# A fused causal attention and expert kernel: score arithmetic, transposes, PSUM banks and the order of the attention rounds changed

## The chip, the cores and the metric

The program runs on one core of a Trainium2 chip. The metric is the device time of one execution in microseconds, the median of three. A second number, the span, is the time from the first to the last instruction of one profiled execution; the rows below belong to that execution.

## The reference

```python
# q, k, v: (4, 12, 448, 64) fp32; w_in: (768, 2048), w_out: (2048, 768), a: (4,), b: (2,)
scores = 1/sqrt(64) * q @ k^T          # causal mask: -1e9 above the diagonal
attn   = exp(scores - max); attn /= sum(attn) + 1e-9
x      = (attn @ v), heads joined      # (1792, 768)
h      = x @ w_in                      # (1792, 2048)
P      = a0 + a1*h + a2*h^2 + a3*h^3
Q      = 1 + |b0|*|h| + |b1|*h^2
out    = (P / (Q + 1e-6)) @ w_out      # (1792, 768)
```

The expert weights arrive as 64-bit floats (the kernel reads them as pairs of 32-bit words) and are converted on the chip.

## The kernel before

**Attention.** Two heads form a pair `p`; there are 24 pairs (4 batches of 6). The work on a pair is cut into small tasks, and the table `ORDER` writes out one round of the attention: the name of a task, a part number, and `@lag`, the number of pairs by which it trails the round. `attend(p, plan)` runs the table once per round, from round -2 on. Each engine gets its instructions in the order in which the table issues them, so the table sets what each engine waits behind. The tasks are:

- `ld`, `lv`: loads of q, k and v through SP's queue. `q` and `k` transpose them on PE (L237, L254) into PSUM; `qh`, `kh` on ACT and `ql`, `kl` on DVE take them out as a high and a low fp32r part.
- `s.0` to `s.3` (`stage_b_pe`, L274): scores of four query blocks, each as three fp32r products (high by high, high by low, low by high). `s.0`, `s.1`, `s.2` make one product per head with 64 rows of the array (widths 128, 256, 384); `s.3` takes the last 64 queries of both heads together with all 128 rows (width 448).
- `m.i` on DVE (mask and row maximum), `e.i` on ACT (exponential with its row sum), `r` on DVE (reciprocal of the sums), `n.i` on POOL (normalisation of `E`, two sets of buffers).
- `c.0` to `c.3` (`c_pe`, L330): 16 transposes of normalised `E` tiles with all 128 rows; `a.n` (ACT) or `v.n` (DVE) copies each of the four results out, 512 columns at a time.
- `d.c` (`stage_d`, L353): fp32 products with v, 64 output columns of the array per head, 1024 columns a head in all; `dh`, `dl` write the high and low part of `x`.
- `cv` (`conv`): converting weights, two DVE and two POOL steps per item; 14 items (`NC`) are converted during the attention and the other 18 later, one per unit of the expert part.

**PSUM.** `ps_t` holds four banks in rotation for all transposes and for `d`; `ps_s` holds four in rotation for the scores.

**Expert part.** 64 units, each `p1` (18 products into `psH`), an elementwise chain on ACT and DVE, and `p2` (products into `psO` and `psM`). The list `TAIL` is the hand-written passage from the last rounds to the first units `p1.0` to `p2.0`; a loop over units follows.

Of the kernel before, what the change touches and what calls it, by code (L numbers as in the profile page):

```python
# [18 lines left out]
e.0 m.1 m.2 e.1 v.0@2 cv.3 k@-1 n.0@1 ld@-2 n.4@1 m.3 lv@1 e.2 n.3@1 n.6@1 s.3 cv.2@-1 qh@-1 a.3@2 kh@-1 s.2  # L19
n.2@1 n.1@1 d.0@2 e.3 m.6 m.4 d.3@2 n.5@1 e.6 m.5 e.4 ql@-1 d.1@2 d.2@2 cv.0@-2 dh@2 c.2@1 e.5 kl@-1 dl@2 c.1@1  # L20
cv.1@-2 s.0@-1 s.1@-1 a.2@1 c.0@1 m.0@-1 c.3@1 q@-2 r a.1@1
# [3 lines left out]
NHEAD = -2  # L25
# [12 lines left out]
def kernel(  # L38
# [27 lines left out]
    NC = 14  # L66
# [123 lines left out]
    def p1(t):  # L190
# [3 lines left out]
        for n, (w, x) in enumerate(((wih, xh), (wih, xl), (wil, xh))):  # L194
            for c in range(KD):
# [8 lines left out]
    raw, K, AT, pv, SUM, REC, psa, pss, psc, nmx, msk, xf = {}, {}, {}, {}, {}, {}, {}, {}, {}, {}, {}, {}  # L204

    def stage_load(p):
# [4 lines left out]
        t = raw[p]["q"] = ld.tile([P, 3, 2, D], F32, tag="q", name="qraw")  # L211
        for j in range(2):
            src = q[b, 2 * hp + j]
            nc.sync.dma_start(out=t[:, :, j], in_=src[:3 * P].rearrange("(c p) d -> p c d", p=P))
            nc.sync.dma_start(out=Q6[p % 2][half(j), j], in_=src[3 * P:])
        t = raw[p]["k"] = ld.tile([CP, NB, 2, D], F32, tag="k", name="kraw")
        for j in range(2):
            nc.sync.dma_start(
                out=t[:, :, j], in_=k[b, 2 * hp + j].rearrange("(c p) d -> p c d", p=CP)
            )  # L220

    def stage_load_v(p):
        b, hp = divmod(p, HP)
        t = V[p % 2]
        for j in range(2):
# [4 lines left out]
            out=t[:QB, :, 3], in_=v[b, 2 * hp:2 * hp + 2, 3 * P:].rearrange("j p d -> p j d")  # L230
# [55 lines left out]

    def stage_b_max(p, i):
# [5 lines left out]
        s = pss[p, i][:, :w]  # L293
# [21 lines left out]
    def stage_b_norm(p, i):  # L315
        e = E[p % 2][i][:, :b_w[i]]
# [396 lines left out]
```

## Time and profile before

| what | us |
|---|---|
| time, median of 3 (lowest, highest) | 667.59 (667.17, 668.99) |
| the profiled execution, its own time | 666.24 |
| its span | 664.5 |
| PE busy, share of the span | 644.9, 97% |
| DVE busy | 536.4, 81% |
| ACT busy | 431.9, 65% |
| POOL busy | 217.7, 33% |

Busy times are averages over stages with different limits; the rows further down take the attention, the passage and the expert part apart. PE is TensorE's matmul side, PEld its weight loads, DVE VectorE, ACT ScalarE, POOL GpSimd, SP the engine that issues the transfers.

### The profile page before, as it was taken

The page shows a single profiled execution, that of the slowest core. Times are in us where ns is not written, and L with a number is a line of the kernel's source. Part 1 is how long each engine was busy: PE and PEld are TensorE (multiplying, and loading weights), DVE is VectorE, ACT ScalarE, POOL GpSimd, SP SyncE. Part 2 cuts the span into 40 slices and gives each one's busy share as a digit, 9 for nine tenths or more (in the row PEclk, how much of TensorE's full clock was granted, in tenths as well). Part 3 has the DMA queues.
Part 4 walks back from the last instruction along what each step waited for, and adds up shares of the span by engine and source line. Part 5 has one row for each costly group of instructions (what it writes and reads, how often), then busy time and mean ns, then how long its engine had stood idle before and what let it go on. Part 6 is the DMA issues. An engine that isn't in the chain of part 4 may idle for free.

```text
span 664.5 us, 11697 instructions
## 1 busy us (share of the span) xinstructions
PE 644.9 (97%) x3960; PEld 541.6 (82%) x3960; DVE 536.4 (81%) x1060; ACT 431.9 (65%) x944; POOL 217.7 (33%) x271
## 2 busy tenths in 40 slices
PE   5999999999989999999999999999999999999997
PEld 3767767767658888788888888889999999999996
DVE  3899999999649999999999968767885666885654
ACT  4798999989766665555656657554564455665453
POOL 3677877785827552243554210000000000000000
PEclk9899999999999999999999999999999999999999
DMA  7679877898507989788696888754757775747753
GB/s 186 168 188 230 234 184 216 197 256 217 169 24 253 311 314 359 267 292 282 231 327 238 283 308 307 265 191 174 273 168 253 249 244 207 256 172 247 258 209 118
DMA packets 111675, 154.91 MB, mean 233 GB/s; under 512 B 71936, under 2 KB 84224, under 8 KB 111616
## 3 DMA queue, kind: packets, MB, share of 16 engines
q1 hardware_dynamic: 111616, 154.17, 71.0%
q8 instruction: 31, 0.51, 0.3%
q14 instruction: 28, 0.23, 0.1%
HBM read 117.18 MB, written 36.96 MB: 232 GB/s over the span
## 4 chain that ended last, share of the span: by engine, by line
PE 71%; DVE 19%; issue 5%; POOL 2%; ACT 2%; SPq 0%; DMA 0%; DVEq 0%; ACTq 0%; POOLq 0%
PE psH L196 23%; PE psO L511 16%; PE psM L512 8%; PE psS L282 8%; PE psD L359 6%; PE psC L340 5%; DVE u L138 3%; DVE p L471 3%; DVE p L465 3%; DVE whl L179 2%; DVE w L462 2%; DVE w L440 2%; POOL e L317 2%; DVE p L443 2%; PE psA L257 1%
## 5 line engine op out<-in xcount | busy, mean ns | idle before, releaser
L196 PE MATMUL psH<-xh,whl 128*128 128x512 f32 (+1 forms) x768 | 175.8, 364 | 0.0
L511 PE MATMUL psO<-whl,gh 128*128 128x512 f32 x448 | 160.4, 394 | 2.3 <-ACT gh L477 2.3
L196 PEld LDWEIGHTS psH<-xh,whl 128*128 128x128 f32 x768 | 136.0, 188 | 15.4 <-issue 0.3
L512 PE MATMUL psM<-whl,gh 128*128 128x256 f32 x448 | 126.2, 282 | 0.0
L317 POOL TENSOR_SCALAR e<-e,r 128x128 f32<-128x128 f32 (+3 forms) x168 | 95.9, 590 | 39.2 <-PE psC L340 20.8
L511 PEld LDWEIGHTS psO<-whl,gh 128*128 128x128 f32 x448 | 84.0, 188 | 22.8 <-ACT gh L477 5.8
L455 ACT ACTIVATE u<-w,lnb 128x512 f32<-128x512 f32 (+1 forms) x64 | 43.0, 672 | 90.6 <-DVE w L440 90.6
L302 ACT ACTIVATE e<-psS,nm 128x128 f32<-128x128 f32 (+3 forms) x168 | 83.2, 507 | 12.8 <-DVE sums L310 5.3
L196 PE MATMUL psH<-xl,whl 128*128 128x512 f32 (+1 forms) x384 | 87.5, 362 | 0.0
L512 PEld LDWEIGHTS psM<-whl,gh 128*128 128x128 f32 x448 | 84.6, 189 | 1.0
L295 DVE CUSTOM_DVE_ANT_0 psS<-psS,mask 128x128 f32<-128x128 f32 (+3 forms) x168 | 73.7, 467 | 11.5 <-PE psS L282 10.3
L511 PE MATMUL psO<-whl,gl 128*128 128x512 f32 x224 | 81.1, 391 | 0.0
L196 PEld LDWEIGHTS psH<-xl,whl 128*128 128x128 f32 x384 | 70.1, 188 | 7.5
L477 ACT CAST gh<-p 128x512 fp32r<-128x512 f32 (+1 forms) x64 | 36.8, 575 | 48.2 <-DVE p L471 48.2
L484 DVE TENSOR_TENSOR gl<-p,gh 128x384 fp32r<-128x384 f32 (+1 forms) x62 | 38.2, 617 | 34.7 <-ACT gh L477 34.7
L433 ACT ACTIVATE u<-psH 128x512 f32<-128x512 f32 (+1 forms) x64 | 34.3, 536 | 46.7 <-PE psH L196 46.6
L512 PE MATMUL psM<-whl,gl 128*128 128x256 f32 x224 | 63.2, 282 | 0.0
L179 DVE TENSOR_TENSOR whl<-w,whl 128x768 fp32r<-128x768 f32 x45 | 44.2, 983 | 22.8 <-ACT whl L171 22.3
L179 POOL TENSOR_TENSOR whl<-w,whl 128x768 fp32r<-128x768 f32 x19 | 41.7, 2196 | 56.3 <-ACT whl L171 53.3
L130 POOL TENSOR_SCALAR raw<-raw 128x768 f32<-128x768 f32 x32 | 38.8, 1214 | 59.1 <-DMA raw<-in_moe_w_out_dram 22.7
L282 PE MATMUL psS<-khl,qh 64*128 64x128 f32 (+3 forms) x336 | 54.0, 354 | 3.3 <-DVE khl L266 2.3
L171 ACT CAST whl<-w 128x768 fp32r<-128x768 f32 x64 | 53.6, 839 | 4.5 <-PE psH L196 4.3
(65 smaller groups left out, 1146.2 us busy)
## 6 DMA issues: line engine op xcount, KB each, us to landing
whl<-whl SPq DMA_DIRECT2D x88, 768.0 KB, 4.2
w<-w SPq DMA_DIRECT2D x64, 384.0 KB, 5.1
raw<-in_moe_w_in_dram SPq DMA_DIRECT2D x16, 768.0 KB, 5.2
w<-u SPq DMA_DIRECT2D x32, 384.0 KB, 2.9
raw<-in_moe_w_out_dram SPq DMA_DIRECT2D x16, 768.0 KB, 5.1
kraw<-in_k_dram SPq DMA_DIRECT2D x48, 112.0 KB, 3.8
out_dram<-osb SPq DMA_DIRECT2D x14, 384.0 KB, 2.8
qraw<-in_q_dram SPq DMA_DIRECT2D x48, 96.0 KB, 4.4
```

The lines of the kernel that those rows point to most:

```text
L130: nc.gpsimd.tensor_scalar(out=y, in0=y, scalar1=2.0 ** -112, scalar2=1.0, op0=ALU.mult, op1=ALU.mult)
L171: nc.scalar.copy(out=w[:, 0], in_=src)
L179: eng.tensor_tensor(out=w[:, 1], in0=src, in1=w[:, 0].bitcast(F32), op=ALU.subtract)
L196: nc.tensor.matmul(ps, w[:, c * P:(c + 1) * P], x[c][:, lo:lo + n_tok], start=(c == 0 and n == 0), stop=(c == KD - 1 and n == 2),)
L282: nc.tensor.matmul(ps[j][:, :w], a[p % 2][d, i * P:(i + 1) * P], K[p][d, b, :w], start=(n == 0), stop=(n == 2), skip_group_check=True,)
L295: nc.vector.tensor_tensor_reduce(out=s, in0=s, in1=m, scale=-1.0, scalar=3e38, op0=ALU.add, op1=ALU.min, accum_out=nmx[p][:, i:i + 1],)
L302: nc.scalar.activation(out=E[p % 2][i][:, :w], in_=pss[p, i][:, :w], func=AF.Exp, bias=nmx[p][:, i:i + 1], scale=-1.0, accum_out=SUM[p][:, ...
L317: nc.gpsimd.tensor_scalar(out=e, in0=e, scalar1=REC[p][:, i:i + 1], scalar2=0.0, op0=ALU.mult, op1=ALU.add)
L359: nc.tensor.matmul(ps[half(j), c * P:S], V[p % 2][:, j, c], AT[p, h][:, j, lo:lo + S - c * P], start=(c == 0), stop=(c == 2), skip_group_c ...
L455: nc.scalar.activation(out=r, in_=w, func=AF.Ln, scale=2.0 ** -LSH, bias=lnb[:, 0:1])
L511: nc.tensor.matmul(acc[k], g, w[:, :512], start=first, stop=last)
L512: nc.tensor.matmul(m, g, w[:, 512:], start=first and k % 2 == 0, stop=last, skip_group_check=True)
```

## The change

Scores become one fp32 product each instead of three fp32r products, so q and k are kept once, as fp32 (`Q`, `K`), and `ql` and `kl` are gone. q is loaded like k, in four chunks of 112 rows; `q_ev` writes it out in three ACT instructions. The transposes of `E` for the first 384 queries are made from halves of 64 rows (`c.0`, `c.1`, 12 instructions each, the two halves into two different banks `t0` and `t1`); the last 64 queries of both heads are transposed whole (`i`, four instructions into bank `t2`) and copied by `ai`. The products with v are issued in seven pieces a head instead of four, with the same 1024 columns. Every PSUM bank is a tile of its own: `t0`, `t1`, `t2`, two for `s.1` (which `s.0` shares), two for `s.2`, one for `s.3`. `E` has three sets of buffers instead of two.

`ORDER` and `TAIL` are written anew; `NHEAD` goes from -2 to -1. One weight item fewer is converted in the attention (`NC` 13): two steps a round in rounds 1 to 4, one a round from 5 to 22. In `TAIL`, `pi` puts the transposes `i` of pairs 22 and 23 inside `p1.0` and `p1.1`, and one of two weight splits moves out of the rounds into `TAIL`.

```diff
-e.0 m.1 m.2 e.1 v.0@2 cv.3 k@-1 n.0@1 ld@-2 n.4@1 m.3 lv@1 e.2 n.3@1 n.6@1 s.3 cv.2@-1 qh@-1 a.3@2 kh@-1 s.2
...
+q@-1 dh@3 k@-1 lv@1 qh@-1 dl@3 s.3 kh@-1 ld@-3 m.3@1 i@2 e.2@1 cv.3 m.6 e.3@1 c.0@2 s.2 e.6 r@1 v.0@2 n.0@1 s.1
+a.0@2 m.5 n.6@1 ai@2 s.0 c.1@2 m.4 n.1@1 e.5 m.0 n.4@1 v.1@2 a.1@2 n.2@1 e.4 m.1 m.2 d@2 n.3@1 e.0 cv.1 cv.2
...
-NHEAD = -2
+NHEAD = -1
...
-    NC = 14
+    NC = 13
...
+    def q_ev(p):
+        nc.scalar.activation(
+            out=Q[p % 2][:, :3 * P], in_=psa[p, 0][:, :3 * P], func=AF.Copy, scale=SCALE
+        )
+        for j in range(2):
+            nc.scalar.activation(
+                out=Q[p % 2][half(j), 3 * P + j * QB:3 * P + (j + 1) * QB], in_=psa[p, 0][half(j), 3 * P:S],
+                func=AF.Copy, scale=SCALE,
+            )
...
-        for n, (a, b) in enumerate(((QH, 0), (QH, 1), (QL, 0))):
-            for j in range(len(ps)):
-                d = half(j) if i < 3 else slice(None)
-                nc.tensor.matmul(
-                    ps[j][:, :w], a[p % 2][d, i * P:(i + 1) * P], K[p][d, b, :w],
-                    start=(n == 0), stop=(n == 2), skip_group_check=True,
-                )
+            d = half(j) if i < 3 else slice(None)
+            nc.tensor.matmul(
+                o, Q[p % 2][d, i * P:(i + 1) * P], K[p][d, :w], start=True, stop=True, skip_group_check=True
+            )
...
+    c_parts = (((0, 0), (0, 1), (0, 2)), ((1, 1), (1, 2), (2, 2)))
+
+    def c_pe(p, h):
+        ps = psc[p, h] = [ps_t.tile([P, 512], F32, tag=f"t{x}", name="psC") for x in range(2)]
+        for j in range(2):
+            for n, (c, i) in enumerate(c_parts[h]):
+                lo = (j * 3 + n) * QB
+                for x in range(2):
+                    r = slice(x * QB, (x + 1) * QB)
+                    nc.tensor.transpose(
+                        ps[x][:, lo:lo + QB], E[p % 3][2 * i + j][r, c * P:(c + 1) * P], ident[r, r]
+                    )
...
+        jobs = [(0, 0, 3 * P, lambda j: a[p, 0][:, j])]
+        jobs += [(c, 3 * P, S, lambda j, c=c: a[p, "i"][:, c, j]) for c in range(4)]
+        jobs += [(1, P, 3 * P, lambda j: a[p, 1][:, j, :2]), (2, 2 * P, 3 * P, lambda j: a[p, 1][:, j, 2])]
...
-        return 2 if p % 3 == 1 else 1
+        return 2 if 1 <= p < 5 else int(5 <= p < NP - 1)
...
-        ps_t = es_l.enter_context(pool(name="ps_t", bufs=4, space=PSUM))
+        ps_t = es_l.enter_context(pool(name="ps_t", bufs=1, space=PSUM))
...
-            if p >= NP - 2:
-                split_w(p - NP + 2, 0)
             attend(p, plan)
+            if p == NP - 2:
+                split_w(0, 0)
```

PE's order in a steady round of the kernel before, from the transposes of k on (psA holds transposes of q and k, psS scores, psD products with v, psC transposes of `E`):

```order
L257 MATMUL psA<-ident,kraw 128x112 x4
L282 MATMUL psS<-khl,qh_195 128x448 x2
L282 MATMUL psS<-khl,ql_197 128x448
L282 MATMUL psS<-khl,qh_195 128x384 x4
L282 MATMUL psS<-khl,ql_197 128x384 x2
L359 MATMUL psD<-at,vraw_201 64x448 x2
L359 MATMUL psD<-at,vraw_201 64x64 x2
L359 MATMUL psD<-at,vraw_201 64x320 x2
L359 MATMUL psD<-at,vraw_201 64x192 x2
L340 MATMUL psC<-ident,e_204 128x128
L340 MATMUL psC<-ident,e_205 128x128
```

PE's order in a steady round of the changed kernel, from the transposes of q on (psI holds the four whole transposes `i`):

```order
L236 MATMUL psA<-ident,qraw 128x112 x4
L236 MATMUL psA<-ident,kraw 128x112 x4
L267 MATMUL psS<-kt,qt_199 128x448
L335 MATMUL psI<-ident,e_216 128x128 x4
L317 MATMUL psC<-ident,e_210 128x64 x2
L317 MATMUL psC<-ident,e_212 128x64 x2
L317 MATMUL psC<-ident,e_214 128x64 x2
L317 MATMUL psC<-ident,e_211 128x64 x2
L317 MATMUL psC<-ident,e_213 128x64 x2
L317 MATMUL psC<-ident,e_215 128x64 x2
L267 MATMUL psS<-kt,qt_199 128x384 x2
L267 MATMUL psS<-kt,qt_199 128x256 x2
```

Work with all 128 rows (q, k, `s.3`, `i`) now stands together, then all work in halves of 64 rows (`c.0`, `s.2`, `s.1`, `s.0`, `c.1`), then the products with v; before, a round went through 128 rows, 64 rows, products with v, 128 rows, 64 rows and back.

ACT's order in a steady round of the kernel before, from the high part of q on (at is the transposed `E`, xh the high part of `x`):

```order
L246 ACTIVATE qh_195<-psA 128x512
L349 COPY at<-psC 128x2x256
L263 CAST khl<-psA 128x448
L302 ACTIVATE e_205,sums<-psS,nm 128x256
L302 ACTIVATE e_208,sums<-psS,nm 128x448
L302 ACTIVATE e_206,sums<-psS,nm 128x384
L369 CAST xh_76<-psD 128x448
L302 ACTIVATE e_207,sums<-psS,nm 128x384
L349 COPY at<-psC 128x2x256 x2
```

ACT's order in a steady round of the changed kernel, from the high part of `x` on:

```order
L364 CAST xh_75<-psD 128x448
L241 ACTIVATE qt_200<-psA 128x384
L245 ACTIVATE qt_200<-psA 64x64 x2
L252 COPY kt<-psA 128x448
L286 ACTIVATE e_205,sums<-psS,nm 128x256
L286 ACTIVATE e_206,sums<-psS,nm 128x256
L286 ACTIVATE e_216,sums<-psS,nm 128x448
L327 COPY at<-psC 128x6x64
L339 COPY ati<-psI 128x512
```

One copy of 512 columns for q becomes three instructions, three copies of transposed `E` become two of 384 columns and one of 512, and the exponentials `e.2` and `e.3` of a pair move into the next round.

## Rows read from the trace of the kernel before

**Rows 1.** The page, slices of the span: granted PE clock (9 is full).

```profile
PEclk9899999999999999999999999999999999999999
```

**Rows 2.** Busy time by stretch: head, 21 rounds, passage, expert part in two.

```profile
core 0: us, PE busy (x) PEld busy (x) DVE busy (x) ACT busy (x) POOL busy (x), PEclk, DMA share, GB/s
27.77:175.76 147.99, 147.43 (x1274) 106.58 (x1273) 138.57 (x447) 134.84 (x422) 109.44 (x173) 1.00 0.84 218
175.76:201.88 26.12, 22.86 (x137) 16.29 (x135) 12.29 (x24) 16.35 (x32) 12.31 (x18) 1.00 0.14 42
0.00:27.77 27.77, 18.85 (x113) 14.23 (x115) 14.61 (x53) 15.91 (x48) 11.93 (x31) 0.94 0.65 157
201.88:358.50 156.62, 154.58 (x782) 130.26 (x781) 155.72 (x183) 92.25 (x143) 75.34 (x48) 1.00 0.83 293
```

**Rows 3.** Timeline of PE, one round: start, length, line, tiles, form, count.

```profile
101.21 0.44 PE L282 MATMUL psS<-khl,qh 64*128 64x128 f32 x4
...
102.09 0.66 PE L340 MATMUL psC<-ident,e 128*128 128x128 f32 x4
...
103.02 0.49 PE L240 MATMUL psA<-ident,qraw 128*128 128x128 f32 x3
103.35 0.27 PE L243 MATMUL psA<-ident,qraw 128*128 128x128 f32 x1
...
103.78 0.66 PE L282 MATMUL psS<-khl,qh 128*128 128x448 f32 x2
...
104.57 0.61 PE L282 MATMUL psS<-khl,qh 64*128 64x384 f32 x4
...
105.28 1.95 PE L359 MATMUL psD<-at,vraw 128*64 128x448 f32 x16
107.17 0.87 PE L340 MATMUL psC<-ident,e 128*128 128x128 f32 x6
```

**Rows 4.** Chain of waits in order of time: one unit's 18 products.

```profile
408.21 4.09 PE psH L196 x18
```

**Rows 5.** Timeline of ACT, one round (idle time before in brackets).

```profile
109.49 0.37 ACT L302 ACTIVATE e<-psS,nm 128x128 f32<-128x128 f32 x1
...
109.85 0.36 ACT L302 ACTIVATE e<-psS,nm 128x128 f32<-128x128 f32 x1
...
110.64 0.60 ACT L246 ACTIVATE qh<-psA 128x512 fp32r<-128x512 f32 x1
111.14 0.58 ACT L349 COPY at<-psC 128x512 f32<-128x512 f32 x1
111.60 0.55 ACT L263 CAST khl<-psA 128x448 fp32r<-128x448 f32 x1
112.03 0.50 ACT L302 ACTIVATE e<-psS,nm 128x256 f32<-128x256 f32 x1
...
114.29 0.53 ACT L369 CAST xh<-psD 128x448 fp32r<-128x448 f32 x1 [0.48 <-PE psD L359]
```

**Rows 6.** Groups of instructions by line (busy us, mean ns): DVE's removed ones.

```profile
L249 DVE SCALAR_TENSOR_TENSOR ql<-psA,qh 128x512 fp32r<-128x512 f32 x24 | 16.4, 685 | 5.1 <-ACT qh L246 5.1
L266 DVE TENSOR_TENSOR khl<-psA,khl 128x448 fp32r<-128x448 f32 x24 | 14.7, 614 | 1.3 <-ACT khl L263 1.3
```

**Rows 7.** Timeline of PE in the passage: waits between the transposes and products.

```profile
186.31 1.09 PE L359 MATMUL psD<-at,vraw 128*64 128x320 f32 x8 [0.39 <-ACT at L349]
...
189.46 0.33 PE L335 MATMUL psC<-ident,e 128*128 128x128 f32 x1 [0.61 <-DVE xl L372]
...
196.63 1.08 PE L359 MATMUL psD<-at,vraw 128*64 128x320 f32 x8 [1.39 <-ACT at L349]
```

**Rows 8.** Timeline of the head: PE's first work, SP's issues.

```profile
0.73 0.44 SPq L214 DMA_DIRECT2D qraw<-in_q_dram  x1
...
3.00 1.12 SPq L218 DMA_DIRECT2D kraw<-in_k_dram  x2
...
6.42 0.98 PE L257 MATMUL psA<-ident,kraw 112*128 112x112 f32 x4 [1.08 <-DMA kraw<-in_k_dram]
```

More of the change, by code (lines that the diff above doesn't have):

```diff
@@ L194, in p1 @@
         for n, (w, x) in enumerate(((wih, xh), (wih, xl), (wil, xh))):
+            if n == 2 and mid is not None:
+                mid()
             for c in range(KD):
@@ L210, in stage_load @@
         raw[p] = {}
[L211 to L219, printed above, removed]
-            )
+        for n, src in (("q", q), ("k", k)):
+            t = raw[p][n] = ld.tile([CP, NB, 2, D], F32, tag=n, name=f"{n}raw")
+            for j in range(2):
+                nc.sync.dma_start(out=t[:, :, j], in_=src[b, 2 * hp + j].rearrange("(c p) d -> p c d", p=CP))
     def stage_load_v(p):
@@ new lines, in c_pe, with c_ev @@
+    def c_pe(p, h):
+        ps = psc[p, h] = [ps_t.tile([P, 512], F32, tag=f"t{x}", name="psC") for x in range(2)]
+        for j in range(2):
+            for n, (c, i) in enumerate(c_parts[h]):
[5 more added lines that the diff above has]
+                    )
+    def c_ev(p, h, x):
+        if (p, h) not in AT:
+            AT[p, h] = at.tile([P, 2, 3, 2, QB], F32, tag=f"at{h}", name="at")
+        o = AT[p, h].rearrange("p j n x q -> p (j n) x q")[:, :, x]
+        i = psc[p, h][x][:, :6 * QB].rearrange("p (n q) -> p n q", q=QB)
+        if x == 0:
+            nc.scalar.copy(out=o, in_=i)
+        else:
+            nc.vector.tensor_copy(out=o, in_=i)
@@ new lines, in i_pe, with i_ev, stage_d @@
+    def i_pe(p):
+        ps = psc[p, "i"] = ps_t.tile([P, 512], F32, tag="t2", name="psI")
+        for c in range(4):
+            lo = min(c * P, S - P)
+            nc.tensor.transpose(ps[:, c * P:(c + 1) * P], E[p % 3][6][:, lo:lo + P], ident)
+    def i_ev(p):
+        AT[p, "i"] = at.tile([P, 4, 2, QB], F32, tag="ati", name="ati")
+        nc.scalar.copy(out=AT[p, "i"].rearrange("p c j q -> p (c j q)"), in_=psc.pop((p, "i")))
+    def stage_d(p):
+        ps = pv[p] = ps_t.tile([P, 512], F32, tag="t2", name="psD")
+        a, v = AT, V[p % 2]
+        jobs = [(0, 0, 3 * P, lambda j: a[p, 0][:, j])]
+        jobs += [(c, 3 * P, S, lambda j, c=c: a[p, "i"][:, c, j]) for c in range(4)]
+        jobs += [(1, P, 3 * P, lambda j: a[p, 1][:, j, :2]), (2, 2 * P, 3 * P, lambda j: a[p, 1][:, j, 2])]
+        for n, (c, lo, hi, src) in enumerate(jobs):
+            for j in range(2):
+                x = src(j)
+                if len(x.shape) == 4:
+                    x = x.rearrange("p n x q -> p (n x q)")
+                elif len(x.shape) == 3:
+                    x = x.rearrange("p x q -> p (x q)")
+                nc.tensor.matmul(
+                    ps[half(j), lo:hi], v[:, j, c], x, start=(n == 0), stop=(n == len(jobs) - 1),
+                    skip_group_check=True,
+                )
@@ L376, in quota @@
     def quota(p):
-        if not 2 <= p < 23:
-            return 0
-        return 2 if p % 3 == 1 else 1
+        return 2 if 1 <= p < 5 else int(5 <= p < NP - 1)
     steps = [(m, n) for m in range(NC) for n in (2, 3)]
```

122 lines of the change are left out of this document (38 added, 84 removed).

## The prediction, made before the changed kernel ran

> **What bounds the kernel now.** I read the busy time by stretch first, then one attention round on each engine, then the two ends of the attention.
>
> The first product with v (pair 0) starts at 27.77 us and that of pair 21 at 175.76, 21 rounds later: 147.99 / 21 = 7.05 us a round [rows 2]. In this stretch PE is busy 147.43 of 147.99 us, at a granted clock of 1.00, which is the 2.4 GHz level [rows 2]. Per round the others are busy: ACT 134.84 / 21 = 6.42 us, DVE 6.60, POOL 5.21 [rows 2]. So PE sets the round, and ACT is only 0.6 us behind it: whatever PE gains beyond 0.6 us a round, ACT does not let through. ACT's only wait worth naming is 0.48 us at the end of the products with v [rows 5], which is that same distance.
>
> The passage, from pair 21's products to the first `p2` at 201.88, takes 26.12 us with PE busy 22.86 [rows 2]; the holes are PE waiting for ACT's or DVE's copies of transposed tiles: 0.39, 0.61 and 1.39 us [rows 7]. The head takes 27.77 us with PE busy 18.85 [rows 2]. After 201.88 the kernels are the same but for one weight item; DVE is busy 155.72 of 156.62 us up to 358.50 [rows 2].
>
> **Unit prices.** A unit of 18 products of 512 columns takes 4.09 us [rows 4], 0.227 us each, 545 clocks at 2.4 GHz: an fp32r product costs about one clock a column. The products with v, which are fp32, run from 105.28 to 107.17, 1.89 us [rows 3], for 1024 columns a head, the two heads side by side: at four clocks a column that is 1.71, and 0.18 is left for the change of array mode. Three whole transposes start in 0.33 us (103.02 to 103.35) [rows 3], 0.11 each, two clocks a column. Before, a round changes mode five times, after, three times.
>
> **PE's round after the change.**
> - q and k: 8 transposes of 112 columns, 8 x 0.11 x 112/128 = 0.76.
> - `i`: 4 x 0.11 = 0.43.
> - `s.3`: 448 columns x 4 clocks = 0.75.
> - `s.2`, `s.1`, `s.0`: 384 + 256 + 128 = 768 columns, both heads side by side in the row halves, x 4 clocks = 1.28. That two row halves run side by side today I take from `s.2`: 3 passes x 384 columns from 104.57 to 105.28 [rows 3], 0.71 us, where one after the other they would need 0.96 without a mode change.
> - `c.0`, `c.1`: 24 half transposes of 64 columns, in 12 side-by-side pairs. No row shows one. Below, half a whole transpose: 12 x 0.055 = 0.66. Above, no gain from the shorter width: 12 x 0.11 = 1.32. I take 0.66, since the score products show pairing and the whole transposes cost by columns.
> - products with v: the same 1024 columns, 1.71, and 0.1 for more pieces.
> - three mode changes x 0.18 = 0.54.
>
> Sum 6.23 us. The same prices give the round before: scores 3 x 768 + 3 x 448 clocks = 1.52, twelve plus four transposes of `E` 1.76, q and k 0.82, products with v 1.71, five changes 0.90, together 6.71 against 7.05 measured. The 0.34 missing lies in narrow fp32r passes (`s.0` takes 0.88 us with `s.1`, from 101.21 to 102.09 [rows 3], where columns alone ask 0.48 and the mode change 0.18); those passes go, so I carry 0.1 over: PE 6.33.
>
> **ACT's round.** Removed: the q copy, 0.50 us (110.64 to 111.14), and three copies of 512 columns, 0.46 (111.14 to 111.60) to 0.53, together 2.0 [rows 5]. Added: q as 384 columns, 0.37 (0.43 for 448, 111.60 to 112.03 [rows 5], scaled); two copies of 64 columns; two of 384, 0.74; one of 512, 0.48. No row shows a 64-column copy: below, its columns at the rate above, 0.06; above, an exponential of 128 columns, 0.36 (109.49 to 109.85) [rows 5]; I take 0.15, near the scaled copy. Added 1.89; ACT 6.42 - 2.0 + 1.89 = 6.3 us (6.1 to 6.7).
>
> **DVE and POOL.** `ql` and `kl` go, 0.69 + 0.61 [rows 6]; one copy of 512 becomes two of 384, about +0.35. DVE falls to about 5.7 us; rounds 1 to 4 hold two conversion steps each, about one more microsecond, and reach 6.6. POOL's work is unchanged, 5.2. Neither sets the round. The cover for DVE is thin in one place: `i` of the next round needs bank `t2`, which `dl` frees on DVE about 1.5 us after the products with v end (ACT's `dh` 0.43, `dl` 0.61 like the `kl` of [rows 6], and two hand-overs that I put at 0.2 to 0.25 each), while q, k and `s.3` keep PE busy for 0.18 + 0.76 + 0.75 = 1.69.
>
> **Banks.** Each is now used by one tile at a time. Walking one round from the end of the products with v (0): q and k end at 0.94, `s.3` at 1.69, `i` 2.12, `c.0` 2.96, `s.0` 4.24, `c.1` 4.57, products with v 4.75 to 6.5 less the part of the mode changes counted twice, about 6.3. ACT: `dh` to 0.67, q and k copied by 1.9 (before `c.0` at 2.3, which overwrites their banks), `e.2` and `e.3` 2.8, `e.6` 3.4, `a.0` 3.8 (before `c.1` at 4.2), `ai` 4.3, `e.5` waiting for DVE to about 5.0, `a.1` 5.4, `e.4`, `e.0`, `e.1` 6.6. The last two pieces of the products with v need `a.1` at about 5.5. So the chain closes on itself at 6.3 to 6.6, both engines waiting a little for each other: I take **6.45 us a round**, bounds 6.2 (both loops ideal) and 6.85 (half transposes at 0.11). 21 rounds: 21 x (7.05 - 6.45) = **12.6 us gained** (4 to 18).
>
> **Head.** Four transfers instead of six stand before pair 0's last k; SP issued the first at 0.73 and k's pair at 3.00 and about 3.56, and PE began on k at 6.42 [rows 8]; two issues of about 0.55 fewer make it 1.1 us earlier. Behind that, `kh` and `kl` no longer stand between the transposes and the scores, and rounds 0 and 1 hold no normalised work. I estimate pair 0's products with v at about 24.3 instead of 27.77: **3.5 gained** (1 to 5). Against it: two conversion items are started sooner and share the transfers with q and k.
>
> **Passage.** PE's work after pair 21's products: 3 x 4.09 for `p1.0` to `p1.2`, two times (0.66 + 0.43 + 1.81) for pairs 22 and 23, and nine mode changes x 0.18, together 19.7. Before, 26.12 - 1.89 = 24.2. The holes shrink, since `i` lies inside the `p1` units and the first pieces of the products with v need only `a.0` and `ai`; but `p1.0` must wait for a score bank of pair 23, about 1.5 us, and I leave 0.7 for the rest: 21.9, **2.3 gained** (0 to 4).
>
> **Expert part.** One item more on DVE, in a stretch that runs 156.62 us for 18.5 units of 8.26 us at full pace (two x 4.09 and a little, as at 408.21 [rows 4]), or 152.8: 3.8 us over for 18 items, **0.2 lost** (0 to 0.6).
>
> **Sum.** 666.24 - 12.6 - 3.5 - 2.3 + 0.2 = 648.0 for the profiled execution, which lay 1.35 under the median: **649.4 us**, 2.7% faster.
>
> **The rivals.**
> - *The weight load of a half transpose is not hidden.* Then each of the 12 pairs costs 0.11, PE's round 6.95 with the carried 0.1; the 21 rounds at about 6.95 give 649.4 + 21 x 0.5 = 660. Against it: whole transposes, each with a weight load of its own, start every 0.11 us, the time of their columns alone [rows 3]. The Trainium skill ("TensorE: Matmul & The Clock Gate", Part 3, the mechanism) says that a weight load overlaps a running product only when its row group differs; the next pair's loads here go to row groups that are in use, so by that rule the rival would hold; the trace speaks against the rule, since loads into all 128 rows overlap there. Chance 0.13.
> - *Row halves do not pair in fp32 or in transposes.* The scores cost 1.28 more and the half transposes 0.66 more: PE 8.27 a round, over 21 rounds and about one round's worth in the passage 649.4 + 22 x 1.82 = 689, slower. It decides from a round of about 7.3, where the gains of both ends are used up. For it: no row shows an fp32 product or a transpose with 64 rows. Against it: fp32r pairs in the row halves and fp32 in the column halves of the products with v. Chance 0.08.
> - *ACT and the single banks bind.* 64-column copies at 0.36 and waits between ACT and PE as long as ACT's 0.48 now: round 6.8, 657. Chance 0.11.
> - *The order does not bring what it says.* The rounds shorten, but head and passage gain nothing, since new waits replace the old: 655. Chance 0.1.
> - *Better.* A round of 6.2 and a passage without holes: 642. Chance 0.08.
>
> The forecast holds the other 0.5.
>
> **How the numbers follow.** The forecast's own range, from rounds of 6.3 to 6.6 and both ends, is 645 to 654. The range that should hold the time 8 times in 10 reaches to the first, third, fourth and fifth rivals: 641 to 661. A measurement of this kernel can tell about 0.3% (2 us) from no change. Slower by more than that: the second rival and a little, 0.09. Within: 0.03, a round near 6.9 with both ends failing. Faster: 0.88.
>
> **What would show it.** In the profile of the changed kernel: starts of products with v 6.45 us apart (6.95 says the first rival, over 8 the second); half transposes starting in pairs, 0.055 us a pair; PE busy below 97% of the rounds while ACT's gaps shrink under 0.3 us; pair 0's products at about 24; 22 us from the end of pair 21's to `p2.0`. The prediction fails if the granted clock leaves 1.00 in the rounds (it is full there now [rows 1]), since every PE term would double.

## The result, and the profile after

The changed kernel takes 660.25 us (658.03 to 661.45 in four executions), the kernel before, run beside it, 667.38: a ratio of 0.9888, 95% interval 0.9854 to 0.9921. It is faster by 1.1%, inside the predicted range, but the predicted 649.4 us, 2.7%, was more than twice the gain. The profiled execution took 660.03 us with a span of 658.2, against 664.5. So 6.3 us of span went where 18.2 were forecast:

| part | before, us | after, us | gained | forecast |
|---|---|---|---|---|
| head, to pair 0's products with v | 27.77 | 26.46 | 1.3 | 3.5 |
| 21 rounds | 147.99 | 144.10 | 3.9 | 12.6 |
| passage, to the first `p2` | 26.12 | 22.46 | 3.7 | 2.3 |
| expert part, to the end | 462.6 | 465.2 | -2.6 | -0.2 |

Busy time by stretch in the changed kernel, as [rows 2] (columns: length, PE, PEld, DVE, ACT and POOL busy with their instructions, granted clock, DMA share, GB/s): the head, the first four rounds, sixteen steady ones, the last, the passage:

```profile
0.00:26.46 26.46, 18.38 (x102) 11.58 (x102) 11.47 (x42) 15.53 (x49) 12.12 (x29) 0.94 0.92 200
26.46:55.88 29.42, 26.53 (x315) 18.57 (x313) 27.53 (x85) 26.89 (x90) 23.18 (x37) 1.00 0.85 233
55.88:163.31 107.43, 107.19 (x1252) 76.48 (x1248) 92.55 (x321) 103.33 (x353) 78.79 (x127) 1.00 0.78 198
163.31:170.56 7.25, 5.77 (x74) 3.90 (x70) 5.98 (x21) 6.29 (x20) 6.22 (x10) 1.00 0.23 71
170.56:193.02 22.46, 21.85 (x198) 16.32 (x195) 12.90 (x29) 16.15 (x36) 12.24 (x16) 1.00 0.44 137
```

A steady round takes 107.43 / 16 = 6.71 us where 6.45 was forecast. That is 4.2 of the missing 8.7 us; the first four rounds (29.42 instead of 4 x 6.45) miss 3.6 and the last one 0.8. (The forecast's 21.9 us for the passage count from the end of pair 21's products; from there, 172.48, the changed kernel needs 20.5.)

In three of the first four rounds PE waits ahead of `i` for `dl`, in front of which two conversion steps stand on DVE: 0.91, 0.73 and 0.87 us. The first of these on PE:

```profile
31.21 0.63 PE L335 MATMUL psI<-ident,e 128*128 128x128 f32 x4 [0.91 <-DVE xl L367]
```

The fourth round has no such wait. There POOL, ahead of the normalisations, waited 1.92 us for raw weights, and twelve half transposes that need normalised `E` took 1.27 us (52.80 to 54.07), 0.85 more than in a steady round.

One steady round on PE, as [rows 3] (start, length, line, tiles, shapes, count):

```profile
103.00 0.87 PE L354 MATMUL psD<-at,vraw 128*64 128x384 f32 x4
103.69 0.64 PE L354 MATMUL psD<-ati,vraw 128*64 128x64 f32 x16
104.22 0.87 PE L354 MATMUL psD<-at,vraw 128*64 128x256 f32 x8
105.03 0.60 PE L236 MATMUL psA<-ident,qraw 112*128 112x112 f32 x4
105.47 0.55 PE L236 MATMUL psA<-ident,kraw 112*128 112x112 f32 x4
105.85 0.93 PE L267 MATMUL psS<-kt,qt 128*128 128x448 f32 x2
106.79 0.63 PE L335 MATMUL psI<-ident,e 128*128 128x128 f32 x4
107.35 0.58 PE L317 MATMUL psC<-ident,e 64*128 64x64 f32 x12
107.77 1.52 PE L267 MATMUL psS<-kt,qt 64*128 64x384 f32 x12
109.21 0.59 PE L317 MATMUL psC<-ident,e 64*128 64x64 f32 x12
109.73 0.54 PE L354 MATMUL psD<-at,vraw 128*64 128x384 f32 x2
```

Twelve half transposes start at 107.35 and the scores behind them at 107.77: 0.42 us for six pairs, 0.07 each, not the 0.11 of the first rival; and `s.2` to `s.0` take 1.44 us for the 1.28 that paired row halves ask (one after the other they would need 2.56), so the second rival is out as well. PE's prices held. Yet the row groups look seamless and the window says PE is busy 107.19 of 107.43 us. Short waits lie inside such groups: `s.3` asks 0.75 us for its columns, and `i` starts 0.94 us after it (105.85 to 106.79). What PE waits for is seen in the other engines' rows. ACT, the same round, as [rows 5]:

```profile
102.30 0.62 ACT L339 COPY ati<-psI 128x512 f32<-128x512 f32 x1
103.00 0.58 ACT L286 ACTIVATE e<-psS,nm 128x384 f32<-128x384 f32 x1
...
104.40 0.21 ACT L286 ACTIVATION_READ_ACCUMULATOR e<-psS,nm 128x1 f32 x1
104.76 0.37 ACT L286 ACTIVATE e<-psS,nm 128x128 f32<-128x128 f32 x1
...
106.25 0.44 ACT L245 ACTIVATE qt<-psA 64x64 f32<-64x64 f32 x2
```

After `ati` the next instruction can start about 0.48 us on, at 102.78, and after the accumulator read 0.10 on, at 104.50. `e.5` starts at 103.00 and `e.0` at 104.76: ACT waits 0.22 and 0.26 us in a round, and works 6.71 - 0.48 = 6.23, against the 6.3 forecast. Both waits are for DVE. DVE's rows:

```profile
101.47 0.17 DVE L294 SCALAR_TENSOR_TENSOR sums<-sums 128x7 f32<-128x7 f32 x1 [0.58 <-ACT e L286]
...
101.86 0.51 DVE L329 COPY at<-psC 128x384 f32<-128x384 f32 x1
102.29 0.56 DVE L279 CUSTOM_DVE_ANT_0 psS<-psS,mask 128x384 f32<-128x384 f32 x1
...
104.20 0.47 DVE L279 CUSTOM_DVE_ANT_0 psS<-psS,mask 128x256 f32<-128x256 f32 x1
104.58 0.14 DVE L279 DVE_READ_ACCUMULATOR2_ANT nm<- 128x1 f32 x1
104.58 1.19 DVE L138 SCALAR_TENSOR_TENSOR u<-raw,u 128x768 uint32<-128x768 uint32 x1
```

`r` (L294) waits 0.58 us for ACT's `e.3`, and behind it in DVE's queue stand `v.0` and the maximum `m.5`, on which ACT's `e.5` waits. And `e.0` starts just after `m.2` (at 104.20, read out at 104.58) is done, though it needs only `m.0`: `s.0` and `s.1` share a bank, `m.2` rewrites `s.1`'s half of it in place, and the program orders the two accesses. ACT waits for DVE, which waits for ACT.

The head, as [rows 8], on SP and PE:

```profile
4.90 1.08 SPq L116 DMA_DIRECT2D raw<-in_moe_w_in_dram  x2
...
14.24 0.58 PE L236 MATMUL psA<-ident,qraw 112*128 112x112 f32 x4 [1.19 <-DMA qraw<-in_q_dram]
15.45 0.57 PE L236 MATMUL psA<-ident,kraw 112*128 112x112 f32 x4 [0.63 <-DMA kraw<-in_k_dram]
15.86 4.07 PE L267 MATMUL psS<-kt,qt 128*128 128x448 f32 x14
```

and the window from 15 to 20 us, with the second of these waits in it:

```profile
15.00:20.00 5.00, 4.55 (x19) 2.46 (x20) 2.33 (x9) 3.17 (x11) 1.40 (x4) 0.66 1.10 174
```

Two loads of raw weights, 768 KB each, go out ahead of pair 2's q and k; PE waits 1.19 and 0.63 us for these, and the granted clock is 0.66 on the mean of that window. In the passage the holes of [rows 7] are gone but for 0.61 us.

### The profile page after: what moved, and what is told of

Its sections match the earlier page's. It is cut to its first block, busy times and chain, and to the rows that moved or that the text cites. A ratio compares the mean times of both kernels' runs of the same rounds, so it can differ in the third digit from the quotient of the medians.

```text
span 658.2 us, 12399 instructions
## 1 busy us (share of the span) xinstructions
PE 636.1 (97%) x4368; PEld 531.3 (81%) x4368; DVE 526.8 (80%) x1036; ACT 434.5 (66%) x992; POOL 219.5 (33%) x269
## 4 chain that ended last, share of the span: by engine, by line
PE 63%; DVE 24%; issue 5%; ACT 4%; POOL 2%; DMA 1%; SPq 1%; DVEq 0%; POOLq 0%; ACTq 0%
PE psH L198 22%; PE psO L504 16%; PE psM L505 8%; PE psS L267 5%; PE psD L354 5%; DVE u L138 3%; DVE w L433 3%; DVE p L464 3%; PE psC L317 3%; DVE p L458 2%; DVE whl L179 2%; DVE w L455 2%; PE psA L236 2%; DVE gl L477 2%; PE psI L335 2%
## 5 line engine op out<-in xcount | busy, mean ns | idle before, releaser
L279 DVE CUSTOM_DVE_ANT_0 psS<-psS,mask 128x128 f32<-128x128 f32 (+3 forms) x168 | 72.0, 477 | 15.4 <-PE psS L267 13.2
L477 DVE TENSOR_TENSOR gl<-p,gh 128x384 fp32r<-128x384 f32 (+1 forms) x62 | 40.0, 645 | 34.9 <-ACT gh L470 34.9
L130 POOL TENSOR_SCALAR raw<-raw 128x768 f32<-128x768 f32 x32 | 41.1, 1284 | 67.5 <-DMA raw<-in_moe_w_in_dram 35.6
L267 PE MATMUL psS<-kt,qt 64*128 64x256 f32 (+3 forms) x336 | 62.6, 428 | 0.0
L179 DVE TENSOR_TENSOR whl<-w,whl 128x768 fp32r<-128x768 f32 x45 | 45.0, 1000 | 21.1 <-ACT whl L171 21.1
L433 DVE SCALAR_TENSOR_TENSOR w<-w,bb,u 128x512 f32<-128x512 f32 (+1 forms) x64 | 53.5, 835 | 3.3 <-ACT w L427 3.3
```

Of the source, the lines that this page charges most:

```text
L130: nc.gpsimd.tensor_scalar(out=y, in0=y, scalar1=2.0 ** -112, scalar2=1.0, op0=ALU.mult, op1=ALU.mult)
L179: eng.tensor_tensor(out=w[:, 1], in0=src, in1=w[:, 0].bitcast(F32), op=ALU.subtract)
L267: nc.tensor.matmul(o, Q[p % 2][d, i * P:(i + 1) * P], K[p][d, :w], start=True, stop=True, skip_group_check=True)
L279: nc.vector.tensor_tensor_reduce(out=s, in0=s, in1=m, scale=-1.0, scalar=3e38, op0=ALU.add, op1=ALU.min, accum_out=nmx[p][:, i:i + 1],)
L433: nc.vector.scalar_tensor_tensor(out=w, in0=w, scalar=bb[:, 0:1], in1=u, op0=ALU.add, op1=ALU.mult)
L477: eng.tensor_tensor(out=gl, in0=pp, in1=gh.bitcast(F32), op=ALU.subtract)
```

## Experiments: what sets the steady round

My theory: PE's own work is 6.3 us, as priced, and the round is the loop of ACT and DVE, 6.23 us of ACT and its two waits. Rivals: PE needs 6.7 itself; or bank `t2`, handed from `dl` to `i`, sets the round. Totals of single runs vary by some 3 us here, so single runs are read by their stretches.

**r@1 behind v.0@2.**

```diff
-... s.2 e.6 r@1 v.0@2 n.0@1 s.1
+... s.2 e.6 v.0@2 r@1 n.0@1 s.1
```

> One edit of the changed kernel: in ORDER the reciprocal r@1 stands behind the copy v.0@2, so that DVE no longer waits 0.58 us for ACT's e.3 ahead of v.0, m.5, m.4 and m.0. Theory 1: DVE's chain to m.5 and m.2 runs about 0.4 us earlier, ACT's waits ahead of e.5 (0.22) and e.0 (0.3) shrink, the round falls to 6.3 to 6.5. Theory 2 (PE needs 6.7 us) and theory 3 (bank t2): the round stays at 6.70.

Measured: sixteen steady rounds in 104.65 us, 6.54 each (one of them 6.89), 656.76 us in one run. Two names swapped gain 2.8 us over these rounds, so PE did not need 6.7.

**e.0 ahead of m.2.**

```diff
-... e.4 m.1 m.2 d@2 n.3@1 e.0 cv.1 cv.2
+... e.4 m.1 e.0 m.2 d@2 n.3@1 cv.1 cv.2
```

> One edit of the changed kernel: in ORDER the exponential e.0 stands ahead of the row maximum m.2 (it waited 0.26 to 0.36 us a round for m.2, with which it shares a tile). Theory 1 (the steady round of 6.70 us is ACT's loop, 6.2 us busy and two waits on DVE, while PE's own work is 6.30): e.0's wait goes, the round falls to about 6.45, the 16 steady rounds from 107.4 to about 103.5 us, the total by 4. Theory 2 (PE itself needs 6.7 us, mode changes and half transposes dearer than priced): the round stays at 6.70. Theory 3 (bank t2, handed from dl to i, sets the round): it stays at 6.70 and PE's wait ahead of i grows.

A miss with a lesson: the steady rounds grew to 111.92 / 16 = 7.00 us, alternating 6.6 and 7.4. DVE's row there:

```profile
100.41 0.43 DVE L279 CUSTOM_DVE_ANT_0 psS<-psS,mask 128x256 f32<-128x256 f32 x1 [0.70 <-ACT e L286]
```

Now `m.2` waits 0.70 us for `e.0`. The conflict over the shared bank has two sides, and the table only chooses who waits; DVE, which then hands on `dl`, is the worse one. That `e.0` and `m.2` depend on each other through the bank is thereby shown.

**Both edits.**

```diff
-... e.6 r@1 v.0@2 ... e.4 m.1 m.2 d@2 n.3@1 e.0 cv.1
+... e.6 v.0@2 r@1 ... e.4 m.1 e.0 m.2 d@2 n.3@1 cv.1
```

> Both edits of ORDER together (r@1 behind v.0@2; e.0 ahead of m.2). Theory 1: a steady round of 6.3 to 6.4 us, PE's own 6.30; 16 rounds about 102 us, total about 655. Theory 2 (PE needs 6.7) and theory 3 (bank t2): 6.70 and 660.

663.78 us (ratio to before 0.9918, 0.9881 to 0.9956), steady rounds 107.68 / 16 = 6.73: the second edit takes back what the first gave. (Its head was longer, too, with pair 0's products at 28.72: PE waited 2.91 us for pair 2's q, and the granted clock was 0.50 from 15 to 20 us.)

**r@1 behind v.0@2, and m.2 ahead of m.1.** If the two must be ordered, `m.2` should come early.

```diff
-... e.4 m.1 m.2 d@2 n.3@1 e.0
+... e.4 m.2 m.1 d@2 n.3@1 e.0
```

> Two edits of ORDER in the changed kernel: r@1 behind v.0@2 (as in the run before that brought the round from 6.70 to 6.52 us), and m.2 ahead of m.1, so that DVE writes s.1's masked scores 0.28 us earlier and ACT's e.0, which shares their bank, waits less. Theory (the round is the loop of ACT and DVE closed by waits, PE's own work 6.30 us): e.0's last wait of 0.18 us goes, the round falls to 6.35 to 6.42, 16 rounds about 102 us, total 654 to 656. Rival (6.52 is already PE with its mode changes): it stays at 6.52, total 657.

```profile
58.00:160.90 102.90, 102.84 (x1252) 75.62 (x1248) 94.44 (x321) 102.08 (x353) 79.75 (x129) 1.00 0.82 205
```

The steady round is 102.90 / 16 = 6.43 us (fifteen of them 6.41 to 6.42, one 6.69), the forecast's 6.45, with the same work on every engine. PE's share reads 99.9% here and 99.8% at 6.71: that share could not tell the two apart. The starts could:

```profile
105.64 0.93 PE L267 MATMUL psS<-kt,qt 128*128 128x448 f32 x2
106.41 0.60 PE L335 MATMUL psI<-ident,e 128*128 128x128 f32 x4
```

From `s.3` to `i` it is 0.77 us here against 0.94 before the two edits. So bank `t2` is not a rival to the loop but the place where it reaches PE: `i` waits for `dl`, `dl` for `dh`, and `dh` stands on ACT behind `e.0`, which had waited for DVE. The rest of the 0.3 us lies mostly in the products with v, 2.03 us (103.00 to 105.03) against 1.91 here. The total, 658.05 us (0.9847, 0.9786 to 0.9907), gained less than these rounds did, since one early round took 9.79 us (below).

**What PE's parts are worth.** The half transposes made whole again, one bank per head (lines joined; the copies out are adapted):

```diff
-                for x in range(2):
-                    r = slice(x * QB, (x + 1) * QB)
-                    nc.tensor.transpose(ps[x][:, lo:lo + QB], E[p % 3][2 * i + j][r, c * P:(c + 1) * P], ident[r, r])
+                nc.tensor.transpose(ps[j][:, n * P:(n + 1) * P], E[p % 3][2 * i + j][:, c * P:(c + 1) * P], ident)
```

> One part of the change undone: the 24 half transposes of c.0 and c.1 (64 rows, 64 columns, in side-by-side pairs) are made as 12 whole ones of 128 rows and 128 columns, one bank per head; the copies out have the same columns. It puts two more mode changes into a round. Theory 1, with half transposes paired and their weight loads hidden (0.061 us a pair, as started in the trace): PE's round grows by 12 x (0.108 - 0.061) = 0.57 and 2 x 0.15 for the modes, 6.30 to 7.15; the round becomes PE's at 7.1 or a little more, 22 rounds x 0.4 = 9 us slower, about 669. Rival (half transposes were not paired or paid for their loads, so that they cost what whole ones do): the round stays at 6.7 to 6.8, total within 3 us of 660.

Sixteen rounds by busy time, and PE's timeline in one of them:

```profile
55.65:167.60 111.95, 111.95 (x1057) 82.09 (x1056) 93.85 (x321) 104.86 (x354) 79.81 (x129) 1.00 0.73 190
```

```profile
108.64 0.82 PE L314 MATMUL psC<-ident,e 128*128 128x128 f32 x6
109.39 1.57 PE L267 MATMUL psS<-kt,qt 64*128 64x384 f32 x12
```

Rounds of 6.99 us, nearly all the same, with no wait left in PE's starts (`s.3` to `i` 0.77 us): now PE sets them. Six whole transposes and the change of mode take 0.75 us (108.64 to 109.39) where twelve halves took 0.42. A round has one mode change more, not two as I had written, since `c.0` now stands beside other work with 128 rows. 666.48 us (0.996, 0.9928 to 0.9993): 5 us slower than the changed kernel by the ratios, 6 by the times, 9 expected.

**FP32 scores alone**, in the kernel before: `ql`, `kl` and the second part of K removed, order and transposes as they were.

```diff
-            for n, (a, b) in enumerate(((QH, 0), (QH, 1), (QL, 0))):
...
+            nc.tensor.matmul(ps[j][:, :w], QH[p % 2][d, i * P:(i + 1) * P], K[p][d, :w], start=True, stop=True, ...)
```

> The kernel before with one part of the change alone: scores as one fp32 product instead of three fp32r ones, without ql and kl; order, whole transposes, banks and head stay as they were. Theory (the fp32 product costs PE 4 clocks a column against 3, so +0.51 us of columns a round, less 0.34 for narrow passes that go; the gain of the change comes from grouping by mode and half transposes): a round of 7.05 to 7.5 us, total 667 to 676. Rival (the lighter DVE and fewer passes carry the gain): the round falls to 6.8 or less, total 662 or less.

```profile
100.34 1.95 PE L358 MATMUL psD<-at,vraw 128*64 128x448 f32 x16
...
107.61 1.95 PE L358 MATMUL psD<-at,vraw 128*64 128x448 f32 x16
```

Twenty rounds of 7.27 us, 0.22 above those before: 670.92 us (1.003, 1.0008 to 1.0053). Taken alone the new scores cost; the halves, with the mode change that they save, are worth 6.99 - 6.43 = 0.56 us a round once the waits are gone (the changed kernel itself, at 6.71, had half of that), and the rest of the new order 7.27 - 6.99 = 0.28. This is a chain of differences between kernels, each read from one profile.

## Experiments: head, early rounds and the ends

**The first raw loads behind pair 2's q and k.**

```diff
-ld@0 ld@1 xd.0 xd.1
+ld@0 ld@1
...
+            if p == 0:
+                conv_load(0)
+                conv_load(1)
```

> One edit of the changed kernel: the two first loads of raw weights (768 KB each) are issued behind the q and k loads of pair 2 instead of ahead of them. Theory (the head lost 1.2 and 0.6 us on PE to q and k of pair 2 that queue behind raw weights): these waits go and pair 0's products with v start near 24.7 instead of 26.46 us; what it saves may come back as later conversion steps (0 to 2 us in the first rounds). Rival (the head is bound by the chain from pair 0's k through scores, maxima and normalisation): the start stays within 0.5 us of 26.46.

Pair 0's products start at 23.67, 2.8 us earlier, though PE's clock is low in this head as well:

```profile
15.00:20.00 5.00, 4.21 (x18) 3.10 (x19) 3.83 (x16) 4.45 (x18) 3.20 (x6) 0.72 0.92 156
```

The 2.8 us are one pair of profiles, and the head varies: in the eight profiles of the changed kernel and its variants with the raw loads ahead, pair 0's products start at 24.1 to 28.7 us (26.1 on the mean), in the six with the raw loads behind at 22.7 to 23.9 (23.4); other edits differ among them. So the issue order is worth about 2.6 us on the mean. The rest was as in the changed kernel (144.19 us for the 21 rounds), 656.48 us in one run.

**Conversion steps spread**, one a round and a second one in rounds 4, 9, 14 and 19:

```diff
-        return 2 if 1 <= p < 5 else int(5 <= p < NP - 1)
+        return 2 if p in (4, 9, 14, 19) else int(1 <= p < NP - 1)
```

> One edit of the changed kernel: the 26 conversion steps are spread as one a round in rounds 1 to 22 and a second one in rounds 4, 9, 14 and 19, instead of two a round in rounds 1 to 4. Theory (a second step of 1.2 us on DVE stands directly ahead of dl, which frees the bank that i waits for, and early on the raw weights come late because of their rate): intervals two to four fall from 7.2 to 7.55 to 6.75, four single intervals later rise by 0.4 to 0.8, net 0 to 2 us faster than the changed kernel, 658 to 660. Rival (the early intervals are long because the rounds start up, q and k included): they stay at 7.2 or more and the late doubles come on top, 662.

The first two rounds fell to 6.67 and 6.73 us (and the head to 24.11), but the four with two steps took 9.02, 10.32, 9.28 and 10.43: 669.82 us (1.0015, 0.9984 to 1.0045). The rows around the second of them, POOL's, DVE's and PE's timeline:

```profile
74.04 0.93 POOL L130 TENSOR_SCALAR raw<-raw 128x768 f32<-128x768 f32 x1 [4.21 <-DMA raw<-in_moe_w_out_dram]
...
76.63 1.13 DVE L138 SCALAR_TENSOR_TENSOR u<-raw,u 128x768 uint32<-128x768 uint32 x1 [0.82 <-POOL u L134]
...
78.44 0.63 PE L335 MATMUL psI<-ident,e 128*128 128x128 f32 x4 [1.38 <-DVE xl L367]
...
79.69 0.73 PE L317 MATMUL psC<-ident,e 64*128 64x64 f32 x8 [0.42 <-POOL e L301]
```

and busy time in short windows, in the first of the four and in this one:

```profile
40.00:42.00 2.00, 1.22 (x7) 0.50 (x5) 2.00 (x4) 1.96 (x8) 2.00 (x2) 1.00 0.52 116
42.00:44.00 2.00, 1.26 (x12) 0.82 (x12) 1.27 (x6) 1.46 (x6) 2.00 (x6) 1.00 0.61 139
44.00:46.60 2.60, 2.26 (x30) 1.74 (x32) 1.52 (x4) 1.21 (x3) 2.60 (x6) 1.00 0.96 258
...
78.00:80.00 2.00, 1.14 (x12) 0.82 (x12) 1.80 (x7) 1.18 (x4) 2.00 (x5) 1.00 0.74 169
...
82.00:84.00 2.00, 2.00 (x22) 1.72 (x20) 1.56 (x7) 0.89 (x4) 2.00 (x4) 0.50 0.74 230
```

Neither theory had this chain in full. The second step uses an item up a round sooner, its raw successor arrives late, and POOL waits 4.21 us for it. From there the delay reaches PE in two ways: DVE's second step waits 0.82 us for POOL and holds up `dl`, so that `i` waits 1.38 us, and the normalisations behind the raw weights in POOL's queue come late, which costs PE 0.42 and 0.29 us. PE stands idle 0.86 of 2 us, and then the granted clock falls to 0.50, the 1.2 GHz level, while PE is busy without a pause. It does not always fall: in the first of the four rounds PE was idle 0.78 and 0.74 of 2 us, and the clock stayed at 1.00. In the third and the fourth PE was busy 0.63 of 2 us each (114 to 116 and 150 to 152 us); after the one the clock stayed, after the other it fell to 0.50. The two rounds in which it stayed took 9.02 and 9.28 us, the two in which it fell 10.32 and 10.43. So the waits make up most of the loss and the clock about 1.2 us; what decides whether it falls, these runs do not show. The 9.79 us round above is like the second: after a POOL wait of 2.66 us PE was busy 1.62 of 2.38 us, and then the scores, 1.52 us elsewhere, took

```profile
48.19 2.60 PE L267 MATMUL psS<-kt,qt 64*128 64x384 f32 x12
```

at a granted clock of 0.56:

```profile
48.19:50.58 2.39, 2.39 (x15) 1.69 (x16) 1.86 (x7) 1.27 (x3) 1.05 (x2) 0.56 0.77 161
```

**Four edits**: `r`, `m.2`, the raw loads, and `cv.3`, which issues the next raw load, at the start of the round.

```diff
-q@-1 dh@3 ... i@2 e.2@1 cv.3 m.6
+cv.3 q@-1 dh@3 ... i@2 e.2@1 m.6
```

> The changed kernel with the edits that gained, together, and one more: r@1 behind v.0@2, m.2 ahead of m.1, the first raw weight loads behind pair 2's q and k, and cv.3 (store of a converted item and load of the next raw one) at the start of the round, so that the raw load is issued some 3.5 us earlier. Theory (steady round 6.41 us as with the first two edits; head of 23.7 us as with the third; POOL's waits of 2.4 to 2.8 us for raw weights in the early rounds made the normalisation late, PE idle and then the granted clock fall to 1.2 GHz, and go with the fourth): pair 0's products near 23.7, four first intervals together 27 to 28.5 us (29.4 in the changed kernel, 31.4 with two edits), 16 steady ones 102.9, total 649 to 652. Rival (the early rounds are long because DVE has two steps in each, whatever POOL waits for): the four stay at 29.4 to 31.4, total 652 to 655.

654.36 us (0.9764, 0.9718 to 0.9811). POOL's waits for raw weights in the early rounds fell to about 1 us and no round was worse than 7.84, but the first four still took 29.94 us, as the rival had it. Two steps a round, 2.2 to 2.4 us ahead of `dl`, hold up `i` by 0.77 us in three of them, which is 2.3 of the 4.3 us over four rounds of 6.41. PE has two more waits there, 0.40 us for `v.1` in the second and 0.78 for ACT's copy in the fourth; their causes are not shown.

**Five edits**, the spread of the conversion steps (its diff above) added to the four:

> As the run with four edits, but the second conversion step of a round stands in rounds 4, 9, 14 and 19 instead of 1 to 4. With the spread alone such a round took 9 to 10.4 us, with 4.2 us of POOL waiting for raw weights in the longest. Theory (it is POOL's wait for raw weights): with the raw load issued 3.5 us earlier such a round falls to 7 to 7.5 us, and the total is within 1 us of the run with four edits. Rival (two steps on DVE by themselves cost 3 us): they stay at 9 us or more, the total 5 us above it.

648.74 us in one run: rounds with one step took 6.41 to 6.47, those with two 6.89 to 6.92 (the last, with the weight split, 6.88). A second step costs 0.5 us here instead of 2.3 to 3.7 with the spread alone. The early raw load is the likely cause, since POOL no longer waits for raw weights in these rounds, but `r` and `m.2` were moved with it. The same kernel in more executions:

> The kernel with five edits (four edits and the spread conversion steps) once more, timed over several rounds, since it had one run of 648.74 us. Theory: a round of 6.41 us, rounds with two steps about 6.9, pair 0's products near 23.7: 648 to 652 us. Rival (that run was a lucky one): 653 to 655 like the run with four edits.

651.65 us (649.07 to 653.42 in six executions), ratio 0.9761, 0.9734 to 0.9787. By stretch (head, the sixteen rounds from the fifth on, passage):

```profile
0.00:22.66 22.66, 16.65 (x102) 10.97 (x102) 9.83 (x41) 15.29 (x50) 9.45 (x27) 0.92 0.88 202
...
48.89:153.11 104.22, 102.89 (x1253) 75.11 (x1249) 96.96 (x324) 102.78 (x353) 83.56 (x131) 1.00 0.90 220
...
159.99:183.12 23.13, 22.20 (x198) 16.60 (x195) 12.99 (x29) 16.14 (x36) 12.98 (x17) 1.00 0.44 136
```

It is the best kernel of this study, 8.6 us below the changed one. Its median lies 2 us above the forecast's 649.4, and its terms lie near the forecast's: head 22.66 (24.3), a round with one step 6.41 (6.45), passage from the end of pair 21's products 21.1 (21.9), expert part 464.2 (462.8).

**The split of weight (0,0) moved into the passage**, to free ACT before pair 21's products (the interval of 7.25 us).

```diff
-            if p == NP - 2:
-                split_w(0, 0)
...
-dl@3 e.2@1 c.0@2 e.3@1 xr
+dl@3 e.2@1 c.0@2 e.3@1 wh.0.0 wl.0.0 xr
```

> As the run with four edits, and the split of weight (0,0) moved out of the rounds into the passage, behind e.3: the interval before pair 21's products lasted 7.25 us against 6.70 because its 0.8 us cast stands ahead of dh on ACT. Theory: that interval falls to 6.5 us, and p1.0 waits no longer than before for its weights: 0.5 us faster than the run with four edits. Rival (the cast only moves: p1.0 now waits for it): the passage grows by as much, no difference.

The interval fell from 6.88 to 6.19 us, but the passage grew from 23.14 to 29.41, 659.86 us in one run:

```profile
153.01 15.13 SPq L162 DMA_DIRECT2D w<-w  x3
...
175.50 1.75 PE L354 MATMUL psD<-at,vraw 128*64 128x384 f32 x4 [4.21 <-DMA vraw<-in_v_dram]
```

A weight load in SP's queue waited for the buffer that the split frees, 15.13 us with its neighbours, and the loads of v stood behind it. The rival had named p1.0's own wait, which was only 1.14 us.

**Fourteen items as before the change**, with early double rounds (the first line added for `quota`) and with the five edits (the second):

```diff
-    NC = 13
+    NC = 14
...
-        return 2 if 1 <= p < 5 else int(5 <= p < NP - 1)
+        return 2 if 1 <= p < 7 else int(7 <= p < NP - 1)
...
+        return 2 if p in (4, 7, 11, 14, 18, 21) else int(1 <= p < NP - 1)
```

> The changed kernel with 14 items converted in the attention (two steps a round in rounds 1 to 6 instead of 1 to 4). Theory (0.2 us an item in the expert part; two more rounds with two steps in a row, each 0.6 us longer and more where raw weights come late): expert part 464 to 466 us, total 0.5 to 3 us above the changed kernel. Rival (the item costs 2.6 us in the expert part, the whole loss seen there): expert part 462.6 as before the change, total within 1 us.

> As the kernel with five edits, but with 14 converted items in the attention as before the change (two more steps, so six rounds with two steps: 4, 7, 11, 14, 18, 21) and the one item fewer in the expert part. Theory (an item in the expert part costs 0.2 us there, as put in the prediction, since DVE has nearly a unit's room): the expert part stays at 463 to 466 us, the rounds grow by 1.0. Rival (DVE is full there and the item costs its two steps, 2 us and more): the expert part falls to 462.5 or less.

The totals were 660.35 and 651.86 us, one run each, as with 13 items. The expert part took 464.2 and 464.3 us with 14 items, 462.6 in the kernel before and 464.1 in the one with fp32 scores alone; with 13 it took 462.9 to 467.9 in twelve executions, the changed kernel's 465.2 among them. Over 22 units in its middle (from the 19th on, where the additional item falls) all four kernels with 14 items need 162.7 us, and the twelve with 13 need 162.7 to 163.7, 163.2 on the mean. So an item costs about 0.5 us there, by my estimate, against my 0.2; the other 2 us of the loss lie in the first 18 units, which take 156.6 us in the one profile before and 156.9 to 161.0 in the others, with 13 items and with 14. What decides that is not shown.

## Why the prediction was right or wrong

- **PE's prices: right.** One fp32 product at four clocks a column, row halves side by side, half transposes at half price, three mode changes: with the waits gone the round is 6.41 to 6.43 us, against 6.33 priced. (The first rival's round, by the same terms, is 6.33 + 0.66 = 6.99, not 6.95.) The rule that I cited from the Trainium skill ("TensorE: Matmul & The Clock Gate", Part 3), that a weight load overlaps a product only in another row group, would have made that rival's 660 us. The measured time is 660, but that is a coincidence: a pair takes 0.07 us, not 0.11, so the trace does not bear the rule out here.
- **Banks: the step that failed first.** I walked a round by when data is ready and stopped ACT once, at `e.5`. I left out the order on DVE, where `r` waits 0.58 us ahead of `v.0` and `m.5`, and the dependence through the bank that `s.0` and `s.1` share. The loop closed at 6.71 instead of 6.45; moving `r` and `m.2` brought it to 6.43. The rival "ACT and the single banks bind" had the place and, with 6.8 us a round, almost the size; of its two conditions ACT's waits came true (0.48 us a round) and the copies at 0.36 did not (0.22). My sign "PE busy below 97%" was no use: the share read 99.8% with the waits in it.
- **DVE and POOL: mis-sized in the double rounds.** I put 6.6 us for DVE and "neither sets the round". Two steps of 1.2 us stand ahead of `dl`, and in three of the first four rounds `i` waits 0.73 to 0.91 us for it; in the fourth POOL's wait for raw weights delays the normalisations behind it: 7.2 to 7.5 us a round, 3.6 us over. Of the early loads I said only that transfers would be shared; I left out what stands behind them in POOL's and DVE's queues.
- **Head: mis-sized.** I counted two issues fewer, and left the raw loads, which I named, without a price. They cost 2.6 us on the mean of the profiles: 26.1 with them ahead of pair 2's q and k and 23.4 with them behind, and 24.3 was forecast.
- **Passage: better than forecast**, 20.5 us from the end of pair 21's products against 21.9, a gain of 3.7 instead of 2.3. The 1.5 us that I put for `p1.0` waiting for a score bank did not appear: `p1.0` follows `c.1` without a wait, and all holes together are 0.61 us. That hid a part of the other misses. **The last round** lost 0.8 us. Most of it is a weight split that the diff moved from the start of the rounds to just ahead of `dh`: away from there, the round was 0.69 us shorter. I did not cost that move.
- **Expert part:** 0.5 for the item against 0.2; the rest varies from profile to profile, and its cause stays open.

## What to carry to other kernels

When an order table is rewritten, walk every engine's queue, not only the data: for each instruction that waits, list what stands behind it and who waits for that. Two tiles in one bank, one of them rewritten in place, tie two engines together, and swapping them in the order only changes who waits; do the rewrite early instead. A late transfer can cost more than its wait when it stands ahead of work that TensorE needs, since the clock may fall afterwards, as it did in two rounds of four here. And compare a forecast with a measurement over the same stretch, from the same first instruction on.

## What was not expected of the hardware

- TensorE's granted clock fell to 0.50 to 0.56 (1.2 GHz) in the midst of the rounds after it had been busy 1.14 of 2.00 and 1.62 of 2.38 us, in pieces of idle time of 1.4 us at most, and the work right after it ran at about 0.6 of its speed: 2.60 us for 1.52. Elsewhere much the same idle time had no such effect (busy 1.22 and 1.26 of 2.00 us, clock 1.00).
- A PE that reads busy 99.8% (107.19 of 107.43 us) did the same work in 4.5 us less once waits on other engines were moved.
- Two 64-column copies on ACT take 0.44 to 0.47 us together, 0.22 to 0.23 each: I had put 0.15.
